# Second MLP's weight pieces loaded from ScalarE's queue, and the decay table loaded between the first q, k and the first k, v

## The chip, the cores and the metric

One core of one Trainium2 chip. The metric is device time in microseconds of one execution, lower is better. The kernel before took 729.98 us, the median of three runs (724.83, 729.98 and 730.90).

## What is computed

Three layers over 2304 tokens of width 512, all in float32 accuracy. The first is retention: attention without a softmax, in which the scores of a head are multiplied by powers of that head's gamma. The second is an MLP (512 to 1024 to 512) with a softmax-like unit and a normalisation in its middle, the third an MLP (512 to 2048 to 512) with a piecewise quadratic unit. Cut to what matters:

```python
scores = scale * q @ k.T                       # 4 batches, 8 heads, 576 tokens, 64 dims
ret = scores * where(i >= j, gamma[h] ** (i - j), 0)
x = heads_joined(ret @ v)                      # 2304 x 512
h = x @ w_in                                   # 512 x 1024
solu = h * softmax(h)
x = ((solu - mean) / sqrt(var + 1e-6) * g_ln) @ w_out
h = x @ moe2_w_in                              # 512 x 2048
g = where(h >= 1, h, where(h <= -1, 0, (h + 1) ** 2 / 4))
out = g @ moe2_w_out                           # 2048 x 512
```

The weights arrive as 64-bit floats, and the kernel turns them into a high and a low 32-bit part itself.

## The kernel before, in words

**Tiles and stages.** The tokens are cut into 18 tiles of 128. Retention runs tile by tile with a running state: `ret_scores` makes the scores (line 115) and multiplies them with the decays inside a tile, `in_sb` (line 124, tile `p`), and scales k by `aft_sb` (line 131); `ret_out` makes the outputs (`po`, lines 143 and 149) and the tile's addition to the state (`pst`, line 170). `mlp1_hidden` multiplies by the first MLP's input weights (`hp`, line 250, twelve matmuls of 512 columns, two halves per token tile; two PSUM buffers), takes a maximum (line 255), and `mlp1_norm` does the softmax and the normalisation: the maxima joined (261), exponentials on ScalarE (265), the product on VectorE (266), which reads `hp` for the last time and so gives its buffer back, and then lines 269 to 283. `mlp1_transpose` (296) and `mlp1_out` (316, 48 matmuls) follow.

**The stretch that the change is about.** A hand-written string, `START`, orders the first steps: L is a load of a tile's q, k (line 104) and k, v (105), C a load of one half of the decays (95), G the other constants, S and O the two retention steps, A and B the first MLP's weights, H and N its hidden and norm. After it a loop runs j from 1 to 8; round j does two token tiles of the first MLP and, in rounds 2 to 5, two tiles of retention. Into the same rounds the second MLP's weights are prepared, in 32 pieces of 512 KB: `prep_load` loads a piece into one of three slots `st` (line 346), and `prep_w2` decodes it: ScalarE copies its two halves (lines 197 and 198), VectorE shifts (199), GpSimd adds (200), VectorE joins (202) and with that the slot is free again; then high and low parts are split off (74 and 75) into a `wi` or `wo` tile, which is stored to DRAM (line 376) for the third layer. `PACE` says how many pieces each of the four places in a round takes. A load of piece k+3 comes right after the decoding of piece k, whose slot it takes.

**What sets the order.** SyncE's instructions stand in the order in which the program makes them, from the first to the last; TensorE's do so from the loop on. ScalarE, VectorE and GpSimd are ordered when the program is built, by a planner that runs the program in a simulated time and takes, of what is ready there, what comes first in the program. At run time every engine goes strictly through its own list. All loads and stores are issued by SyncE, so a load of a piece stands in one row with: the stores of the first MLP's outputs (`store_x2`, line 331, which wait for the splits of `px`), the loads of k, v (105, which wait until `pst` of an earlier tile has read its buffer), and the stores of the prepared weights (376).

**After the rounds** only the second MLP runs (lines 414 to 462), bound by TensorE.

Of the kernel before, what the change touches and what calls it, by code (L numbers as in the profile page):

```python
# [20 lines left out]
B, H, S, D = 4, 8, 576, 64  # L21
T = B * S
DM = H * D
F1, F2 = 1024, 2048
P = 128
# [3 lines left out]
C1, C2 = F1 // P, F2 // P  # L29
# [2 lines left out]
PACE = [[], [0, 0, 0, 0], *[[2, 1, 1, 1]] * 4, *[[2, 2, 1, 1]] * 2, [0, 0, 0, 0]]  # L32

START = """
L0 C1 C0 G0 L1 s0 A0 G1 O0 S1 L2 o1 A1 L3 S2 o2 A2 L4 S3 A3 O3 L5 S4 B0 O4 L6 S5 b1 O5 L7 B2 S6 O6 H0 H1 L8 b3 S7 O7 N0 L9 B4 S8 O8 b5 H2 H3 L10 S9 O9 N1 B6 b7 L11
"""


# [16 lines left out]
def net(ctx: ExitStack, tc: tile.TileContext, qk_t, kv, w_in1, w_out1, g_ln, w_in2, w_out2, inside, before, after, across, out):  # L55
    nc = tc.nc
# [16 lines left out]
    def split(hi, lo, src, eng=nc.vector):  # L73
        nc.scalar.activation(hi, src, AF.Copy)  # L74
        eng.tensor_tensor(out=lo, in0=src, in1=hi.bitcast(F32), op=ALU.subtract)  # L75
# [18 lines left out]
    def load_inside(e):  # L94
        nc.sync.dma_start(in_sb[:, e], inside[:, e])
# [5 lines left out]
    def load_qkv(t):  # L101
        x = raw.tile([P, 2, KD, P], F32, tag="qk", name="qk")
        y = raw.tile([P, 2, H, D], F32, tag="kv", name="kv")
        nc.sync.dma_start(x, qk_t[t])
        nc.sync.dma_start(y, kv[t])
        raws[t] = x, y

# [78 lines left out]
    def words(src, n):  # L186

        return src.bitcast(U32).rearrange("p (f t) -> p f t", t=2)

    def decode(st, tag=None, sb=False, dst=None):  # L190

        lo, hi = st[:, :, 0], st[:, :, 1]
        y = stage.tile([P, 512], U32, tag="y", name="y", bufs=3)
        w = ps.tile([P, 512], U32, tag=tag, name="w") if tag else y
        nc.scalar.activation(w.bitcast(F32), hi.bitcast(F32), AF.Copy, scale=2.0**-112)
        nc.scalar.activation(lo.bitcast(I32), lo, AF.Copy, scale=2.0**-29)  # L198
        nc.vector.tensor_scalar(y, w, 3, None, op0=ALU.logical_shift_left)  # L199
        nc.gpsimd.tensor_tensor(out=y.bitcast(I32), in0=y.bitcast(I32), in1=lo.bitcast(I32), op=ALU.add)  # L200
        r = dst.bitcast(U32) if dst is not None else y if sb else w
        nc.vector.scalar_tensor_tensor(
            out=r, in0=w if tag else hi, scalar=0x80000000, in1=y, op0=ALU.bitwise_and, op1=ALU.bitwise_or
        )
        return r.bitcast(F32)
# [36 lines left out]
    def mlp1_hidden(t, f):  # L242
        xh, xl = x1[t]
        hp = ps.tile([P, 512], F32, tag="o" if t % 2 and (t == 3 or t >= 13) else "h", name="hp")
        fs = slice(f * 512, (f + 1) * 512)
        n = 0
        for kk in range(KD):
            wh, wl = w_in1_sb[kk]
            for a, w in ((xh, wl), (xl, wh), (xh, wh)):
                nc.tensor.matmul(hp, a[:, kk, :], w[:, fs], start=(n == 0), stop=(n == 3 * KD - 1))  # L250
                n += 1
        hps[t, f] = hp
        if f == 0:
            es[t] = (small.tile([P, 12], F32, tag="sm", name="sm"), act1.tile([P, F1], F32, tag=f"e{t % 2}", name="e"))
        nc.vector.tensor_reduce(out=es[t][0][:, f : f + 1], in_=hp, op=ALU.max, axis=AX.X, negate=True)
# [29 lines left out]
    def mlp1_transpose(t):  # L285
        e = es.pop(t)[1]
        if t % 2 == 0:
            ln = act1.tile([P, 2, C1, 2 * P], F32R, tag="ln", name="ln")
            lnT[t // 2] = ln[:, 0], ln[:, 1]
        lh, ll = lnT[t // 2]  # L290
        cols = slice((t % 2) * P, (t % 2 + 1) * P)
        for f4 in range(2):
            tp = ps.tile([P, 4, P], F32, tag="tr", name="tp")
            for j in range(4):
                f = 4 * f4 + j
                nc.tensor.transpose(tp[:, j, :], e[:, f * P : (f + 1) * P], ident)  # L296
            split(lh[:, 4 * f4 : 4 * f4 + 4, cols], ll[:, 4 * f4 : 4 * f4 + 4, cols], tp)
# [31 lines left out]
    def store_x2():  # L329
        for dst, x in xstores:  # L330
            nc.sync.dma_start(dst, x)
        xstores.clear()
# [9 lines left out]
    def prep_load(n):  # L342
        for _ in range(min(n, len(todo))):
            w, i = todo.pop(0)
            st = stage.tile([P, DM, 2], U32, tag="st", name="st")
            nc.sync.dma_start(st, words(w_out2[i * P : (i + 1) * P, :] if w else w_in2[i], DM))
            staged.append((w, i, st))

    def prep_w2(n):

        for _ in range(n):
            w, i, st = staged.pop(0)
            later = [x for x in stores if len(staged) + len(todo) <= x[2] - 2]
            stores[:] = [x for x in stores if x not in later]
            if w == 0:
                x = prep.tile([P, 2, DM], F32R, tag="wi", name="wi", bufs=2)
                split(x[:, 0], x[:, 1], decode(st))
                stores.append((wid[i], x.rearrange("p w (c f) -> p w c f", c=KD), len(staged) + len(todo)))
            elif i % 2 == 0:
                ws[i // 2] = prep.tile([P, 7, 2 * P], F32, tag="ws", name="ws")  # L360
                decode(st, dst=ws[i // 2][:, 0:2].rearrange("p i f -> p (i f)"))
            else:
                y = ws.pop(i // 2)
                decode(st, dst=y[:, 2:4].rearrange("p i f -> p (i f)"))
                for o, a, b in ((4, 1, 0), (1, 3, 1), (5, 3, 4), (6, 2, 5)):
                    nc.gpsimd.tensor_tensor(out=y[:, o], in0=y[:, a], in1=y[:, b], op=ALU.subtract)
                x = prep.tile([P, 2, 7, 2 * P], F32R, tag="wo", name="wo")
                for part in (slice(0, 4), slice(4, 7)):
                    split(x[:, 0, part], x[:, 1, part], y[:, part])
                stores.append((wod[i // 2], x, len(staged) + len(todo)))  # L370
            if len(staged) == 0:
                later += stores
                stores.clear()
            prep_load(1)
            for dst, x, _ in later:
                nc.sync.dma_start(dst, x.bitcast(F32))

# [8 lines left out]
    def load_xs(b, pool):  # L386
        n = blocks[b][1]
        xs[b] = pool.tile([P, 2, KD, n], F32R, tag="ln", name="xs")
        nc.sync.dma_start(xs[b].bitcast(F32), xsd[b])
# [85 lines left out]
    def project_end(b, t):  # L475
# [20 lines left out]

    gs = {}
    start = {
        "L": load_qkv, "C": load_inside, "G": load_consts, "S": ret_scores, "O": ret_out, "A": prep_w_in1, "B": prep_w_out1,
        "H": lambda i: mlp1_hidden(i // 2, i % 2), "N": mlp1_norm, "Y": mlp1_transpose,  # L500
    }
    order = ExitStack()
# [4 lines left out]
    for j in range(1, NT // 2):  # L507
        a = 2 * j
        ra, rb = a + LEAD, a + LEAD + 1
        more = 10 <= ra < NT  # L510
        n = PACE[j]
        mlp1_transpose(a - 2)
        if more:
            ret_scores(ra)
        mlp1_hidden(a, 0)
        mlp1_hidden(a, 1)
        mlp1_norm(a)
        prep_w2(n[0])
        mlp1_transpose(a - 1)
        if more:  # L520
            ret_out(ra)
        prep_w2(n[1])
        store_x2()
        if more:
            ret_scores(rb)
        mlp1_hidden(a + 1, 0)
        mlp1_hidden(a + 1, 1)
        mlp1_norm(a + 1)
        if j == 1:
            pre.close()  # L530
            prep = pre.enter_context(tc.tile_pool(name="prep", bufs=1, side="right", reuse_waits="tile"))
        if more:
            ret_out(rb)
        prep_w2(n[2])
        if more and ra + 2 < NT:
            load_qkv(ra + 2)
        mlp1_out(j - 1, 0)
        if j == 1:
            prep_load(3)
        prep_w2(n[3])  # L540
        if more and rb + 2 < NT:
            load_qkv(rb + 2)
        mlp1_out(j - 1, 1)
        if rb == NT - 1:
            attn.close()
            xsa = ctx.enter_context(tc.tile_pool(name="xsa", bufs=1, side="left", reuse_waits="tile"))
            gsp = ctx.enter_context(tc.tile_pool(name="gsp", bufs=1, side="left", reuse_waits="tile"))
            load_xs(0, xsa)
        if j == 6:
            for c in range(2):  # L550
                load_wi(c, w2a, f"w{c}")
        if j == 7:
            pre.close()
            wos = ctx.enter_context(tc.tile_pool(name="wos", bufs=1, side="right", reuse_waits="tile"))
            for c in range(2, 4):
                load_wi(c, w2a, f"w{c}")
            for s in range(3):
                load_wo(s)
# [78 lines left out]
```

## Time and profile before

| what | value |
|---|---|
| median of three runs | 729.98 us |
| the profiled execution, its own time | 727.76 us |
| its span in the profile | 726.0 us |
| mean granted TensorE clock | 0.979 of full |
| TensorE matmul busy | 688.2 us, 95% |
| VectorE busy | 497.1 us, 68% |
| ScalarE busy | 359.8 us, 50% |
| GpSimd busy | 169.7 us, 23%, all before 330 us |

The profile shows one execution. "Busy" counts computing instructions; issuing a DMA is not counted. An idle stretch is put down to the semaphore that ended it. In a timeline, the bracket at a line's end gives the idle time before the instruction and who ended it. `SPq` and `ACTq` are DMA issues of SyncE and ScalarE; such a line shows the issue, not the transfer. The chain is the work that ended last, followed back from the end.

### The profile page before, as it was taken

The page shows a single profiled execution, that of the slowest core. Times are in us where ns is not written, and L with a number is a line of the kernel's source. Part 1 is how long each engine was busy: PE and PEld are TensorE (multiplying, and loading weights), DVE is VectorE, ACT ScalarE, POOL GpSimd, SP SyncE. Part 2 cuts the span into 40 slices and gives each one's busy share as a digit, 9 for nine tenths or more (in the row PEclk, how much of TensorE's full clock was granted, in tenths as well). Part 3 has the DMA queues.
Part 4 walks back from the last instruction along what each step waited for, and adds up shares of the span by engine and source line. Part 5 has one row for each costly group of instructions (what it writes and reads, how often), then busy time and mean ns, then how long its engine had stood idle before and what let it go on. Part 6 is the DMA issues. An engine that isn't in the chain of part 4 may idle for free.

```text
span 726.0 us, 12169 instructions
## 1 busy us (share of the span) xinstructions
PE 688.2 (95%) x4744; PEld 618.5 (85%) x4744; DVE 497.1 (68%) x961; ACT 359.8 (50%) x658; POOL 169.7 (23%) x186
## 2 busy tenths in 40 slices
PE   5888789998989999999999999999999999999997
PEld 4677578887878889999888989898988899899996
DVE  2977777677588678754566578556865668575875
ACT  2746775575667569763434344333433343343342
POOL 2896645636555235400000000000000000000000
PEclk9989899999999999999999999999999999999999
DMA  8956534487869399699564523346135511555282
GB/s 299 373 185 250 186 116 157 152 324 245 299 224 340 128 356 394 242 391 402 178 242 143 190 89 144 137 184 218 47 125 192 203 59 59 203 193 196 77 320 116
DMA packets 34825, 152.05 MB, mean 209 GB/s; under 512 B 3792, under 2 KB 11984, under 8 KB 29008
## 3 DMA queue, kind: packets, MB, share of 16 engines
q1 hardware_dynamic: 34624, 151.02, 56.8%
q8 instruction: 37, 0.61, 0.3%
q10 hardware_dynamic: 144, 0.26, 0.1%
q14 instruction: 20, 0.16, 0.1%
HBM read 114.04 MB, written 37.22 MB: 208 GB/s over the span
## 4 chain that ended last, share of the span: by engine, by line
PE 72%; DVE 11%; DMA 6%; ACT 4%; POOL 3%; issue 3%; SPq 0%; DVEq 0%; POOLq 0%; ACTq 0%
PE h L414 27%; PE hp L250 9%; PE px L316 7%; PE pa L462 7%; PE pb L462 7%; PE pc L462 7%; PE pd L462 3%; DMA st<-in_w_out 2%; POOL y L200 2%; PE po L149 1%; DMA wod<-wo 1%; PE tp L296 1%; DVE y L199 1%; DVE wo L75 1%; DVE p L124 1%
## 5 line engine op out<-in xcount | busy, mean ns | idle before, releaser
L414 PE MATMUL h<-xs,wi 128*128 128x512 f32 (+1 forms) x960 | 214.2, 372 | 0.0
L414 PEld LDWEIGHTS h<-xs,wi 128*128 128x128 f32 x960 | 163.8, 188 | 28.5
L424 DVE SCALAR_TENSOR_TENSOR r<-r 128x512 f32<-128x512 f32 (+1 forms) x80 | 50.8, 635 | 104.0 <-ACT r L422 103.9
L422 ACT ACTIVATE r<-h 128x512 f32<-128x512 f32 (+1 forms) x80 | 44.4, 555 | 154.7 <-PE h L414 154.6
L74 ACT ACTIVATE gh<-gs 128x1024 fp32r<-128x1024 f32 (+1 forms) x80 | 66.9, 874 | 77.1 <-DVE gs L437 72.9
L316 PE MATMUL px<-ln,wo 128*128 128x256 f32 x864 | 101.4, 278 | 0.0
L316 PEld LDWEIGHTS px<-ln,wo 128*128 128x128 f32 x864 | 100.5, 188 | 0.8 <-ACT e L265 0.2
L250 PE MATMUL hp<-wi1h,x 128*128 128x512 f32 x288 | 96.3, 417 | 0.0
L75 DVE TENSOR_TENSOR gl<-gs,gh 128x1024 fp32r<-128x1024 f32 (+1 forms) x80 | 77.1, 995 | 13.3 <-ACT gh L74 13.2
L200 POOL TENSOR_TENSOR y<-y,st 128x512 int32<-128x512 int32 x48 | 64.2, 1340 | 70.6 <-ACT st L198 22.9
L250 PE MATMUL hp<-wi1l,x 128*128 128x512 f32 x144 | 62.7, 435 | 14.6 <-DVE e L266 12.6
L462 PE MATMUL pb<-wo,gh 128*128 128x256 f32 x288 | 73.9, 280 | 0.4 <-DVE x L75 0.4
L250 PEld LDWEIGHTS hp<-wi1h,x 128*128 128x128 f32 x288 | 58.6, 203 | 13.4
L437 DVE TENSOR_TENSOR gs<-gs 128x256 f32<-128x256 f32 (+1 forms) x160 | 60.0, 396 | 3.6
L462 PE MATMUL pa<-wo,gh 128*128 128x256 f32 x288 | 62.5, 280 | 0.0
L462 PE MATMUL pc<-wo,gh 128*128 128x256 f32 x288 | 62.0, 280 | 0.0
L429 DVE TENSOR_TENSOR gs<-h,r 128x512 f32<-128x512 f32 (+1 forms) x80 | 51.1, 638 | 7.3 <-DVE r L424 0.5
L462 PEld LDWEIGHTS pb<-wo,gh 128*128 128x128 f32 x288 | 54.3, 188 | 0.6 <-issue 0.6
L462 PEld LDWEIGHTS pa<-wo,gh 128*128 128x128 f32 x288 | 49.2, 189 | 2.7
L462 PEld LDWEIGHTS pc<-wo,gh 128*128 128x128 f32 x288 | 49.1, 188 | 0.0
L250 PEld LDWEIGHTS hp<-wi1l,x 128*128 128x128 f32 x144 | 29.4, 204 | 22.6 <-DVE e L266 13.6
L423 ACT COPY h<-h 128x512 f32<-128x512 f32 (+1 forms) x80 | 43.1, 539 | 0.0
(88 smaller groups left out, 1139.0 us busy)
## 6 DMA issues: line engine op xcount, KB each, us to landing
wo<-wod SPq DMA_DIRECT2D x28, 1792.0 KB, 7.4
wod<-wo SPq DMA_DIRECT2D x8, 1792.0 KB, 9.4
st<-in_w_out SPq DMA_DIRECT2D x24, 512.0 KB, 6.1
qk<-in_qk_t SPq DMA_DIRECT2D x18, 512.0 KB, 6.5
kv<-in_kv SPq DMA_DIRECT2D x18, 512.0 KB, 4.5
xsd<-x SPq DMA_DIRECT2D x36, 256.0 KB, 6.4
st<-in_w_in SPq DMA_DIRECT2D x16, 512.0 KB, 6.2
wid<-wi SPq DMA_DIRECT2D x16, 512.0 KB, 7.2
```

Of the source, the lines that this page charges most:

```text
L74: nc.scalar.activation(hi, src, AF.Copy)
L75: eng.tensor_tensor(out=lo, in0=src, in1=hi.bitcast(F32), op=ALU.subtract)
L200: nc.gpsimd.tensor_tensor(out=y.bitcast(I32), in0=y.bitcast(I32), in1=lo.bitcast(I32), op=ALU.add)
L250: nc.tensor.matmul(hp, a[:, kk, :], w[:, fs], start=(n == 0), stop=(n == 3 * KD - 1))
L316: nc.tensor.matmul(px[:, mm, :], w[:, ms], a[:, f, :], start=(n == 0), stop=(n == 3 * C1 - 1))
L414: nc.tensor.matmul(hp[:, :n], wi[c][:, w, kk], xs[b][:, a, kk], start=(k == 0), stop=(k == 3 * KD - 1))
L422: nc.scalar.activation(r[:, :n], hp[:, :n], AF.Relu, bias=0.5, scale=0.5)
L423: nc.scalar.copy(h[:, :n], hp[:, :n])
L424: nc.vector.scalar_tensor_tensor(out=r[:, :n], in0=r[:, :n], scalar=1.0, in1=r[:, :n], op0=ALU.min, op1=ALU.mult)
L429: nc.vector.tensor_tensor(out=g, in0=h_, in1=r_, op=ALU.max)
L437: nc.vector.tensor_tensor(out=g[:, o], in0=g[:, x], in1=g[:, y], op=op)
L462: nc.tensor.matmul(po[key][:, half], a[:, x, t], wo[p][0][:, w, y], start=(begin and j == 0), stop=(last and j == 2), skip_group_check=True,)
```

## The change

Two things. The two halves of the decay table, until now loaded after the first tile's q, k and k, v in the order half 1, half 0, are loaded inside the first tile's load, half 0 then half 1, between q, k and k, v. And the loads of the 32 weight pieces are issued by ScalarE instead of SyncE; two instead of three are issued ahead, and the next one is issued at the beginning of a piece's step instead of after its decoding.

```diff
 START = """
-L0 C1 C0 G0 L1 s0 A0 G1 O0 S1 ...
+L0 G0 L1 s0 A0 G1 O0 S1 ...
 """
@@ load_qkv
         nc.sync.dma_start(x, qk_t[t])
+        for e in range(2 if t == 0 else 0):
+            load_inside(e)
         nc.sync.dma_start(y, kv[t])
@@ prep_load
             st = stage.tile([P, DM, 2], U32, tag="st", name="st")
-            nc.sync.dma_start(st, words(w_out2[i * P : (i + 1) * P, :] if w else w_in2[i], DM))
+            nc.scalar.dma_start(st, words(w_out2[i * P : (i + 1) * P, :] if w else w_in2[i], DM))
             staged.append((w, i, st))
@@ prep_w2
         for _ in range(n):
+            prep_load(1)
             w, i, st = staged.pop(0)
...
             if len(staged) == 0:
                 later += stores
                 stores.clear()
-            prep_load(1)
             for dst, x, _ in later:
                 nc.sync.dma_start(dst, x.bitcast(F32))
@@ start
-        "L": load_qkv, "C": load_inside, "G": load_consts, ...
+        "L": load_qkv, "G": load_consts, ...
@@ the loop over j
         if j == 1:
-            prep_load(3)
+            prep_load(2)
         prep_w2(n[3])
```

## Rows read from the trace of the kernel before

**Rows 1.** The page, fourth part: the chain that ended last, share of the span by engine.
```profile
PE 72%; DVE 11%; DMA 6%; ACT 4%; POOL 3%; issue 3%; SPq 0%; DVEq 0%; POOLq 0%; ACTq 0%
```
**Rows 2.** Busy time by stretch, line 250 alone; after the matmuls: clock, DMA share, GB/s.
```profile
75.00:250.00 175.00, 70.34 (x252) 53.16 (x252) 0.94 0.61 211
250.00:330.00 80.00, 34.89 (x144) 26.60 (x144) 1.00 0.91 350
```
**Rows 3.** Waits of TensorE, whole span: us in total, times, longest.
```profile
PE hp L250 <- DVE e L266: 12.6, 5, 2.8
```
**Rows 4.** The chain that ended last, pieces of 100 to 245 us: start, us, what.
```profile
117.87 5.34 DMA wid<-wi
...
128.56 4.61 PE hp L250 x12
...
139.78 1.18 SPq L346
141.01 9.24 DMA wod<-wo
...
165.21 7.41 PE hp L250 x24
...
237.49 7.41 PE hp L250 x24
```
**Rows 5.** Timeline: SyncE's issues and the VectorE work that frees their slots.
```profile
107.39 1.75 DVE L202 SCALAR_TENSOR_TENSOR ws<-st,y 128x512 uint32<-128x512 uint32 x1
...
109.45 7.86 SPq L331 DMA_DIRECT2D xsd<-x  x4
117.41 0.41 SPq L346 DMA_DIRECT2D st<-in_w_out  x1
...
184.62 7.02 SPq L331 DMA_DIRECT2D xsd<-x  x4
185.24 0.68 DVE L202 SCALAR_TENSOR_TENSOR y<-st,y 128x512 uint32<-128x512 uint32 x1
...
191.73 0.42 SPq L346 DMA_DIRECT2D st<-in_w_in  x1
```
**Rows 6.** Timeline, 196 to 232 us: what follows a late load on three engines.
```profile
196.26 0.68 ACT L197 ACTIVATE y<-st 128x512 f32<-128x512 f32 x1 [5.12 <-DMA st<-in_w_in]
...
197.32 0.68 DVE L255 TENSOR_REDUCE sm<-hp 128x1 f32<-128x512 f32 x1
...
202.36 0.50 PE L250 MATMUL hp<-wi1l,x 128*128 128x512 f32 x1 [2.54 <-DVE e L266]
...
231.44 0.68 ACT L197 ACTIVATE y<-st 128x512 f32<-128x512 f32 x1 [1.24 <-DMA st<-in_w_in]
```
**Rows 7.** The beginning: median landing of DMAs issued before 3 us; chain; timeline.
```profile
kv<-in_kv SPq DMA_DIRECT2D x1, 512.0 KB, 4.5
in_sb<-in_inside SPq DMA_DIRECT2D x2, 256.0 KB, 6.0
...
2.58 5.88 DMA aft_sb<-in_after
...
1.64 0.90 SPq L95 DMA_DIRECT2D in_sb<-in_inside  x2
8.55 0.69 DVE L131 TENSOR_TENSOR kv<-kv,aft_sb 128x512 f32<-128x512 f32 x1 [7.70 <-DMA aft_sb<-in_after]
9.90 0.69 PE L149 MATMUL po<-p,kv 128*64 128x128 f32 x2 [3.28 <-DVE p L124]
14.53 0.33 SPq L105 DMA_DIRECT2D kv<-in_kv  x1
```
**Rows 8.** Waits of ScalarE (78 to 250 us) and of GpSimd (whole span).
```profile
ACT y L197 <- DMA st<-in_w_in: 16.5, 6, 5.1
...
POOL ws L366 <- DVE ws L202: 16.2, 11, 2.5
```
**Rows 9.** Timeline: the only DMA that ScalarE issues before the change.
```profile
722.53 0.38 ACTq L494 DMA_DIRECT2D out<-osb  x1
```

More of the change, by code (lines that the diff above doesn't have):

```diff
@@ L34 @@
 START = """
-L0 C1 C0 G0 L1 s0 A0 G1 O0 S1 L2 o1 A1 L3 S2 o2 A2 L4 S3 A3 O3 L5 S4 B0 O4 L6 S5 b1 O5 L7 B2 S6 O6 H0 H1 L8 b3 S7 O7 N0 L9 B4 S8 O8 b5 H2 H3 L10 S9 O9 N1 B6 b7 L11
+L0 G0 L1 s0 A0 G1 O0 S1 L2 o1 A1 L3 S2 o2 A2 L4 S3 A3 O3 L5 S4 B0 O4 L6 S5 b1 O5 L7 B2 S6 O6 H0 H1 L8 b3 S7 O7 N0 L9 B4 S8 O8 b5 H2 H3 L10 S9 O9 N1 B6 b7 L11
 """
@@ L498, in net @@
     start = {
-        "L": load_qkv, "C": load_inside, "G": load_consts, "S": ret_scores, "O": ret_out, "A": prep_w_in1, "B": prep_w_out1,
+        "L": load_qkv, "G": load_consts, "S": ret_scores, "O": ret_out, "A": prep_w_in1, "B": prep_w_out1,
         "H": lambda i: mlp1_hidden(i // 2, i % 2), "N": mlp1_norm, "Y": mlp1_transpose,
```

## The prediction

> **What bounds the kernel now.** I read the page first. The chain that ended last is TensorE for 72% of the span, VectorE for 11%, transfers for 6%, ScalarE for 4% [rows 1]: the kernel can gain in the 28% where something else holds TensorE up, and where TensorE is slow. The busy time by stretch shows where that is. From 250 us to the end of the first MLP its matmuls follow one another at full clock, 34.89 us for 144, or 0.242 us each; from 75 to 250 us the same 252 matmuls take 70.34 us, 0.279 each, at a granted clock of 0.94 [rows 2]. At the later price they would have taken 61.1, so 9.3 us of that stretch are lost to the lower of the two clock levels. The list of TensorE's waits gives the idle part: five waits, 12.6 us in all and 2.8 at the longest, for VectorE's line 266, which frees the PSUM buffer of `hp` [rows 3]. The chain, read in order of time, shows four of them inside the rounds: TensorE starts again at 128.56, 165.21 and 237.49, each time slowly (4.61 us for 12, 7.41 for 24, where 12 and 24 at the later price take 2.9 and 5.8) [rows 4], and at 202.36 after 2.54 us of idling [rows 6]. The fifth lies ahead of these. Before each gap the chain runs over VectorE, ScalarE, stores and loads of weight pieces, so the preparation of the second MLP's weights is what TensorE ends up waiting for.
>
> Next, the timeline of SyncE's queue. A load needs a free slot, and it needs its turn. The slot of the load issued at 117.41 was freed by the join that began at 107.39 and took 1.75, so at 109.1; the load stood 8.3 us behind four stores of `px` outputs. That of 191.73 had its slot from 185.24 + 0.68 = 185.9 on, and stood 5.8 us behind the next such four [rows 5]. ScalarE then waits for the landing with everything behind it: six waits, 16.5 us [rows 8].
>
> **Start.** The same bytes change places. Now k, v land 4.5 us after an issue just ahead of the decays' 1.64, so near 5.7, and the second half of the decays near 2.1 + 6.0 = 8.1; `aft_sb` lands at 2.58 + 5.88 = 8.46, and VectorE, which has the scaling of k first in its list, begins at 8.55, does the decays behind it and lets `po` begin at 9.90 [rows 7]. With the places changed I expect decays near 6 and k, v near 8.1; VectorE can then multiply the decays in while it waits, and `po` begins when v is there, near 8.3. That is 1.6 us; I take **-1.5**. It is passed on, because the third tile's k, v load stands at 14.53 until `po` has read its buffer [rows 7], and the first weights are issued behind it. Bounds: nothing, if the planner leaves the scaling of k first; +0.9, the issue time of the two halves, if k, v and not `aft_sb` then end that wait.
>
> **Loads off SyncE's queue.** The distance does not change: piece k+2 issued before the decoding of k, and k+3 issued after it, both take the slot that was freed last. What goes is the time behind other transfers. By gaps:
> - 202.36: late load, ScalarE's copy at 196.26 after a wait of 5.12 us, VectorE's shift behind it, and so the second maximum only at 197.32; then exponentials, product, TensorE [rows 6]. With the load issued some 5 us earlier the copy doesn't wait and the gap closes: **-2.5**. Next comes TensorE's own work.
> - 237.49: the copy at 231.44 waited 1.24 us for a load of the same kind [rows 6]; the rest is VectorE's own queue. **-1.2**.
> - 165.21: the chain comes here from a store of prepared weights at 141.01, 9.24 us long, which was issued behind a load that held SyncE for 1.18 [rows 4]. The store stays on SyncE but has no load ahead of it: **-1.2**.
> - 128.56: the chain comes from a store issued at 117.87, behind the load of 117.41 [rows 4, 5]. The four stores before both stay: **-0.5**.
> - Clock: three of these gaps are followed by some 1.7 us of slowness (4.61 against 2.9, 7.41 against 5.8) [rows 2, 4]. I count one of the three as saved, **-1.7**; bounds 0 and -5.0.
>
> Together -7.1. The bounds: 0, if all these gaps have VectorE's queue as their true cause, and all four gaps whole. These are 2.54 where the wait stands [rows 6], for the other three at most 2.8 each [rows 3], and the clock's 5.0: -16.
>
> **What ScalarE pays.** It issues 32 DMAs more. Its only one now takes 0.38 us [rows 9], so 12 us. In the rounds it has idle time of its own to hide them, of which the 16.5 us of waiting for landings alone [rows 8] is more. Behind a load stand the exponentials and splits of its list. ScalarE holds 4% of the chain, 29 us [rows 1], and the rounds and the start, where most of this must lie, last some 330 us: a tenth. A tenth of the 12 us is 1.2; I take **+1.0**, between 0 and 12. The wait for the slot moves to ScalarE as well: for a piece with a following split ScalarE waits for the same join anyway, so it costs little; for the others see the third rival.
>
> After 330 us nothing of the change runs. Behind 250 us TensorE is dense [rows 2], so an earlier start there is kept.
>
> The issuing rule of the Trainium skill speaks against this change: its page "DMA: Bandwidth & Descriptors", section "Issuing engines are not separate DMA queues", says that DMAs started by several engines share the same 16 DMA engines, and that a second issuer saves only the issuing time. By that rule alone the sum would be the second rival's time. No row of this case shows how two issuers share the engines; but the 8.3 and 5.8 us lie before the issue [rows 5], which the rule doesn't count.
>
> **Sum.** -1.5 - 7.1 + 1.0 = -7.6. The profiled execution took 727.76 us itself (726.0 of span and 1.8 around it), which makes 720.2. The runs' median of 729.98 lies 0.3% higher, so 722.4 in its measure; I give **722**. A measurement of this kernel can tell about 1% from no change, 7.3 us, so this stands just at that edge.
>
> **Rivals.**
> 1. *All gaps close.* Once loads come on time, decoding is over before the maxima, and all four gaps go with their clock: 727.76 - 1.5 - 16 = 710.3, in the median's measure 712. For it: every gap is preceded by preparation work. Against: the stores at 117.87 and 141.01, which the chain goes through, stay in SyncE's order. Chance 0.13.
> 2. *The load was hidden anyway.* VectorE's queue and the stores set the gaps, and only the start's 1.5 us stay, less ScalarE's 1.0: 727.3, or 729.5. For it: two of the four gaps come over stores. Against: the straight line from late load to gap at 202.36. That the change doesn't do what it says belongs here: the planner may place the load on ScalarE's list no earlier than SyncE had it. Chance 0.27.
> 3. *ScalarE stands in front of the exponentials.* A load in its list waits until VectorE's join frees the slot, and line 265 waits behind it, which frees `hp`. GpSimd, which waits for that join today, did so 11 times, 16.2 us, 1.5 each [rows 8]. With the issue that is 1.9 us a stand. If two stands per round meet the exponentials in rounds 2 to 5, that is 15.2 and the clock's 5.0 on top, without gain from the loads: 727.76 - 1.5 + 20.2 = 746.5, or 749 in the median's measure; with half of it 739. It decides when ScalarE's waits at its loads exceed the 16.5 us that it now waits for landings. Against: the planner puts the load where the slot is free by its own reckoning. Chance 0.12.
>
> **How the numbers follow.** Forecast 0.48, rivals 0.13, 0.27, 0.12. The range 711 to 739 reaches from the first rival to half of the third; the forecast's own is 716 to 727. Faster by over 1%, that is below 722.7: half of the forecast's cases and the first rival, with some beyond, 0.42. Slower by over 1%: the third rival, 0.12. Within 1%: 0.46.
>
> **What would show it.** Right: ScalarE's waits for `st` landings before 250 us fall from 16.5 us to below 6; loads are issued within 2 us of their slot's join; the gap near 202 is gone, and TensorE's waits for line 266 sum to 6 to 9 us; `po` begins near 8.3 us. Wrong: loads still late, which is the second rival; waits of ScalarE at the new load line of 10 us or more with longer gaps at `hp`, the third; or the gaps as before though the loads come early, which would say that VectorE's queue was the cause.

## The result, and the profile after

The kernel after takes **736.87 us** (median of ten runs, 732.71 to 740.72); the kernel before, in ten runs beside it, 726.7 us. The ratio is 1.0136, with a 95% interval of 1.0106 to 1.0167. The forecast was 722, and faster. The number lies in the range of 711 to 739, but on the wrong side of no change.

The profiled execution of after has a span of 735.0 us, 9.0 more than before. Its page, the engines' busy time, then the landings of the pieces' loads (the last number is the median from issue to landing, in us):

```profile
PE 685.0 (93%) x4744; PEld 615.3 (84%) x4744; DVE 502.7 (68%) x961; ACT 360.4 (49%) x658; POOL 170.2 (23%) x186
...
st<-in_w_in ACTq DMA_DIRECT2D x16, 512.0 KB, 4.5
st<-in_w_out ACTq DMA_DIRECT2D x16, 512.0 KB, 3.9
```

TensorE, ScalarE and GpSimd are busy within 3.2 us of before and VectorE for 5.6 us more; the mean granted clock is 0.985 against 0.979. So TensorE is not slower, it idles more. Before, the loads of these pieces landed 6.2 and 6.5 us after their issue; now 4.5 and 3.9:

```profile
st<-in_w_in SPq DMA_DIRECT2D x16, 512.0 KB, 6.2
st<-in_w_out SPq DMA_DIRECT2D x16, 512.0 KB, 6.5
```

So the edit did what it says, and the loads are quicker. They also leave on time: 27 of the 29 that need a freed slot are issued within 2 us of the join that frees it, where before it was 10.

The loss is made in the rounds: the last `px` matmul starts at 361.7 us, against 352.7 before, which is the whole 9.0; behind it the two kernels run alike. Taken at the first matmul of a tile's `hp`, the changed kernel is still level at 164.8 us (165.2 before), 4.7 us behind at 193.7, 7.2 at 231.6 and 9.4 at 246.9.

TensorE's waits of after from 75 to 330 us (us in total, times, longest):

```profile
PE hp L252 <- DVE e L268: 9.0, 4, 3.2
PE px L318 <- DVE state L179: 5.0, 1, 5.0
PE tp L298 <- ACT e L285: 3.3, 1, 3.3
PE hp L252 <- DVE y L204: 3.2, 2, 2.5
PE tp L298 <- DVE ln L75: 2.7, 3, 1.6
PE tp L298 <- DVE x L75: 2.1, 1, 2.1
PE px L318 <- DVE state L185: 1.2, 1, 1.2
```

Line 268 is line 266 of before; all lines from 105 on are two higher. The sum is 26.5 us, 27.5 with `po`'s, against 16.6 before, where beside the 12.6 of [rows 3] there were only these two:

```profile
PE hp L250 <- DVE y L202: 2.1, 1, 2.1
PE tp L296 <- ACT e L283: 1.9, 1, 1.9
```

The wait for line 266 (now 268) has fallen from 12.6 to 9.0. What has grown are the waits of `px` and `tp`, for the state, for the normalised tile and for splits: 14.3 us together, 1.9 before. And ScalarE, from 75 to 330 us:

```profile
ACT st L200 <- DMA st<-in_w_out: 14.8, 5, 5.4
...
ACT st L200 <- DMA st<-in_w_in: 7.8, 4, 4.2
...
ACT y L199 <- DMA st<-in_w_in: 4.8, 2, 3.7
```

The waits for landings have not fallen. They have moved from a piece's first copy (line 199, 197 before: 21.8 us in this stretch then, most of it in [rows 8]) to its second (line 200, 198 before: 2.0 us then). The second copy works in place on the low words, so it needs no `y` buffer, and nothing can use it until the first copy has run too. In the list of ScalarE's instructions as built, 21 of the second MLP's 32 second copies stand ahead of their own first copy; before it was 5. The planner has laid ScalarE's row anew.

The largest new wait, in the timeline from 161 to 185 us. Each line is start, duration, engine and line; the bracket is the idle time before it and what ended it:

```profile
161.79 0.35 ACTq L348 DMA_DIRECT2D st<-in_w_out  x1
162.25 0.42 SPq L378 DMA_DIRECT2D wod<-wo  x1
162.98 0.33 SPq L104 DMA_DIRECT2D qk<-in_qk_t  x1
164.14 0.33 ACTq L348 DMA_DIRECT2D st<-in_w_in  x1
...
170.85 0.67 ACT L200 ACTIVATE st<-st 128x512 int32<-128x512 uint32 x1 [5.39 <-DMA st<-in_w_out]
171.42 0.71 ACT L275 ACTIVATE junk<-e,sm 128x512 bf16<-128x512 f32 x1
...
176.46 0.67 ACT L200 ACTIVATE st<-st 128x512 int32<-128x512 uint32 x1 [4.23 <-DMA st<-in_w_in]
177.02 0.71 ACT L275 ACTIVATE junk<-e,sm 128x512 bf16<-128x512 f32 x1
177.85 0.21 DVE L279 TENSOR_SCALAR sm<-sm 128x1 f32<-128x1 f32 x1 [7.40 <-ACT junk L275]
...
182.06 0.69 DVE L268 SCALAR_TENSOR_TENSOR e<-hp,e 128x512 f32<-128x512 f32 x1 [2.36 <-ACT e L267]
...
183.47 0.85 DVE L179 COPY state<-pst 64x256 f32<-64x256 f32 x2
...
184.47 7.29 PE L318 MATMUL px<-ln,wo 128*128 128x256 f32 x48 [5.04 <-DVE state L179]
```

Read it upwards. TensorE waits 5.04 us for VectorE to empty `pst`. VectorE stands in its own row 7.40 us at line 279, a step of 0.21 us that adds up the two squares of a normalisation. The squares (line 275) are ScalarE's: the first at 171.42, the second at 177.02, and between them a second copy that waits 4.23 us for a piece. VectorE stands another 2.36 us at line 268 for exponentials that come behind all this in ScalarE's row. Before, nothing stood between that pair of squares:

```profile
169.48 0.72 ACT L273 ACTIVATE junk<-e,sm 128x512 bf16<-128x512 f32 x1
170.33 0.72 ACT L273 ACTIVATE junk<-e,sm 128x512 bf16<-128x512 f32 x1
```

The same happens at 223 us, where two squares are 4.4 us apart with a landing waited for in between. The kernel before has one such pair, at 179 us, 4.35 us apart.

Why the pieces land late just there is in the DMA list, issues from 160 to 166 us:

```profile
wod<-wo SPq DMA_DIRECT2D x1, 1792.0 KB, 14.0
st<-in_w_out ACTq DMA_DIRECT2D x2, 512.0 KB, 6.3
kv<-in_kv SPq DMA_DIRECT2D x1, 512.0 KB, 9.1
qk<-in_qk_t SPq DMA_DIRECT2D x1, 512.0 KB, 14.6
st<-in_w_in ACTq DMA_DIRECT2D x1, 512.0 KB, 12.3
```

The load of 164.14 is issued right after the join that frees its slot (163.43 + 0.68), and lands 12.3 us later, beside a store of 1792 KB and two more pieces. In these 6 us the kernel before issued the same store, q, k and k, v, but one piece where there are now three: 3328 KB against 4352. At the 306 GB/s of the next line 4352 KB take 14.6 us, which is an estimate. DMA share and rate of 162 to 176 us:

```profile
162.00:176.00 14.00, 12.11 (x93) 10.47 (x92) 8.31 (x19) 4.48 (x10) 7.48 (x10) 1.00 0.91 306
```

Before, the same 14 us had a DMA share of 0.69 and 245 GB/s.

### The profile page after: what moved, and what is told of

It is laid out like the page before. It is cut to its first block, busy times and chain, and to the rows that moved or that the text cites. A ratio compares the mean times of both kernels' runs of the same rounds, so it can differ in the third digit from the quotient of the medians.

```text
span 735.0 us, 12160 instructions
## 1 busy us (share of the span) xinstructions
PE 685.0 (93%) x4744; PEld 615.3 (84%) x4744; DVE 502.7 (68%) x961; ACT 360.4 (49%) x658; POOL 170.2 (23%) x186
## 4 chain that ended last, share of the span: by engine, by line
PE 58%; DVE 5%; DMA 2%; ACT 1%; issue 1%; DVEq 0%; SPq 0%; ACTq 0%
PE h L416 27%; PE pa L464 7%; PE pb L464 7%; PE pc L464 7%; PE px L318 4%; PE pd L464 3%; PE hp L252 3%; DMA wod<-wo 2%; PE tp L298 1%; DVE ln L75 1%; DVE gl L75 1%; DVE wo L75 1%; DVE sm L257 1%; DVE ws L204 0%; DVE e L268 0%
## 5 line engine op out<-in xcount | busy, mean ns | idle before, releaser
L318 PE MATMUL px<-ln,wo 128*128 128x256 f32 x864 | 102.9, 280 | 6.2 <-DVE state L179 5.0
L252 PE MATMUL hp<-wi1h,x 128*128 128x512 f32 x288 | 92.3, 402 | 0.0
L75 DVE TENSOR_TENSOR gl<-gs,gh 128x1024 fp32r<-128x1024 f32 (+1 forms) x80 | 77.0, 995 | 13.6 <-ACT gh L74 13.5
L252 PE MATMUL hp<-wi1l,x 128*128 128x512 f32 x144 | 60.1, 418 | 12.4 <-DVE e L268 9.0
L252 PEld LDWEIGHTS hp<-wi1h,x 128*128 128x128 f32 x288 | 55.7, 193 | 12.3
L200 ACT ACTIVATE st<-st 128x512 int32<-128x512 uint32 x48 | 32.1, 671 | 25.1 <-DMA st<-in_w_out 16.0
```

What stands on the lines that cost most here:

```text
L318: nc.tensor.matmul(px[:, mm, :], w[:, ms], a[:, f, :], start=(n == 0), stop=(n == 3 * C1 - 1))
```

## The experiments

Each ratio is to the kernel before, run beside it on the same chip, with its 95% interval. Each version was run ten times, but the loads alone, the loads on GpSimd, the same hold with SyncE, the fourth slot and the held loads four times. "After with" means the changed kernel with one more edit.

### Which part of the change it is

**The start alone.** The decays' order as changed; the pieces' loads stay on SyncE, three ahead.

```diff
-L0 C1 C0 G0 L1 s0 A0 G1 O0 S1 ...
+L0 G0 L1 s0 A0 G1 O0 S1 ...
+        for e in range(2 if t == 0 else 0):
+            load_inside(e)
```

> Only the start's order is changed; the weight pieces are loaded by SyncE as before. Theory A (ScalarE stands at landings that come late, because the planner puts a piece's copies right behind a load that now shares the DMA engines with a store of prepared weights): within 2 us of before, ratio 0.997 to 1.003, waits of ScalarE for st landings between 110 and 250 us near before's 18 us. Theory C (the changed start makes the planner lay out the rounds anew, and that is the loss): +7 to +11 us, ratio 1.010 to 1.015.

Measured: 1.0008 (0.9977 to 1.0039). The start is worth nothing.

**The loads alone.** From ScalarE, two ahead; the start as before.

```diff
-            nc.sync.dma_start(st, ...)
+            nc.scalar.dma_start(st, ...)
+            prep_load(1)
...
-            prep_load(1)
...
-            prep_load(3)
+            prep_load(2)
```

> Only the loads are moved to ScalarE, two ahead; the start is as before. Theory A: +7 to +11 us, ratio 1.010 to 1.015, with single waits of ScalarE for st landings of 4 us or more in the rounds and TensorE waits at px or tp that before has not. Theory C: within 2 us of before.

Measured: 1.0148 (1.0112 to 1.0185), which is the whole loss. ScalarE waits at the second copies again (10.9 + 9.1 us).

**After with the loads on SyncE.** The new place in the step, two ahead, the old queue.

```diff
-            nc.scalar.dma_start(st, ...)
+            nc.sync.dma_start(st, ...)
```

> As the changed kernel, but the loads are issued by SyncE, at the new place (two ahead, before the decoding). Theory A: about before's time, ratio 0.995 to 1.004, since the loads stay in SyncE's row and finish in the order of their issue. Theory D (the new place in the step, not the queue, is the loss): ratio 1.010 or more. If ScalarE's issuing is the loss (theory B), about before's time as well.

Measured: 0.9956 (0.9934 to 0.9978): faster than the kernel before. Only 6 second copies stand ahead of their first, and the waits for landings sit at the first copies (11.5 + 6.0 us). The new place in the step is a gain (from 1.0008 with the start alone), and the queue is the loss. In SyncE's row the new place is a later one: the load that takes the same slot now stands behind the stores of the step before it, where it stood ahead of them. That this is what gains is argued from the program; no run holds the two apart.

**After with the loads on GpSimd.**

```diff
-            nc.scalar.dma_start(st, ...)
+            nc.gpsimd.dma_start(st, ...)
```

> As the changed kernel, but the loads are issued by GpSimd. SyncE's row is as free as with ScalarE, and ScalarE issues nothing. Theory A: the landings are as late and the copies on ScalarE stand as before, so still slower than before, ratio 1.005 to 1.02. Theory B (the 32 issues on ScalarE and its waits for slots are the loss): ratio 1.000 or lower.

Measured: 1.0187 (1.0140 to 1.0235). ScalarE issues nothing here, so its issuing isn't needed for a loss of this size. But the run is no clean mirror. 18 second copies stand early again, and GpSimd itself now stands 34.5 us at the loads, for their slots:

```profile
POOL st L348 <- DVE ws L204: 34.5, 6, 15.0
```

### Where ScalarE stands for a landing

**After with both copies held.** Each of a piece's two copies must stand behind ScalarE's instruction that is traced ahead of it. For the first copy that is the load of the piece two on, for the second it is the first copy.

```diff
-        nc.scalar.activation(w.bitcast(F32), hi.bitcast(F32), ...)
-        nc.scalar.activation(lo.bitcast(I32), lo, ...)
+        first = nc.scalar.activation(w.bitcast(F32), hi.bitcast(F32), ...)
+        if pin: tc.keep_in_program_order(first)
+        second = nc.scalar.activation(lo.bitcast(I32), lo, ...)
+        if pin: tc.keep_in_program_order(second)
```

> As the changed kernel, but in the preparation of the second MLP's weights the two copies of a piece are kept in ScalarE's list behind what the program makes ahead of them, so the planner can't put them in front of a normalisation. Theory L (the list: with loads off SyncE's row the planner takes the pieces as landed early and puts their copies in front of ScalarE's work for the norm, where they stand until the landing): the loss goes, ratio 0.990 to 1.004, and TensorE's waits at px and tp go. Theory S (sharing: loads off SyncE's row land late and make q, k, k, v and stores land late, wherever the copies stand): still 1.008 or more.

Measured: 0.9956 (0.9935 to 0.9977). The loss is gone, with the loads still on ScalarE's queue. ScalarE's waits from 75 to 330 us: the two new ones, which are for a slot (the load ahead of the copy waits for the join that frees it), and the only one left for a landing, which is a copy of the first MLP's weights:

```profile
ACT y L199 <- DVE ws L208: 11.4, 4, 4.2
ACT y L199 <- DVE y L208: 4.5, 2, 3.3
...
ACT w L199 <- DMA st<-in_w_out: 2.2, 1, 2.2
```

TensorE's waits in the same stretch fall to 14.9 us, and none is for the state or a split:

```profile
PE hp L256 <- DVE e L272: 10.6, 5, 3.2
PE hp L256 <- DVE y L208: 3.3, 1, 3.3
PE tp L302 <- ACT e L289: 1.0, 2, 0.6
```

**The same hold, with the loads on SyncE.** Both edits above together.

> The loads issued by SyncE two ahead, with the start of the changed kernel, and the same two copies kept in program order. Theory L: SyncE's row already keeps the pieces near their place, so little changes against the same kernel without it: 0.990 to 1.000 of before. If keeping the order is costly by itself: above 1.004.

Measured: 1.0632 (1.0588 to 1.0676); a clear miss. With no load on ScalarE's list, the first copy is held behind ScalarE's compute of the same step, which comes late. Slots come free late, and SyncE's row stands at the loads, 184.6 us in all from 75 to 330 us (before: 58.0), 45 of them at 85 us, with q, k and k, v behind them; TensorE then waits 11.1 us for q, k. SyncE's three largest waits there (us in total, times, longest), then the longest of its issues:

```profile
SPq L352 <- DVE y L208: 83.9, 7, 44.3
SPq L352 <- DVE ws L208: 54.2, 6, 21.4
SPq L352 <- DVE sm L283: 27.4, 3, 11.8
```
```profile
84.98 45.01 SPq L352 DMA_DIRECT2D st<-in_w_out  x2
```

**After with a fourth slot**, three ahead (another pool gives up a buffer for it).

```diff
-    stage = ...tile_pool(name="stage", bufs=3, ...)
+    stage = ...tile_pool(name="stage", bufs=4, ...)
-    small = ...tile_pool(name="small", bufs=4, ...)
+    small = ...tile_pool(name="small", bufs=3, ...)
-            prep_load(2)
+            prep_load(3)
```

> As the changed kernel with four slots for pieces instead of three, three loads ahead (and three instead of four small tiles of the norm, for room). Theory S, and any theory in which the lead is too short: the pieces are there when the copies come, the loss goes, ratio 0.990 to 1.004. Theory L: the planner uses the lead to put the copies still earlier, and ScalarE stands as long: ratio 1.008 to 1.02.

Measured: 1.0247 (1.0191 to 1.0302). More lead makes it worse: 30 of 32 second copies now stand early. If late loads were the trouble, a slot more should have helped. The small tile that the norm lost could cost as well, and no run took it away alone; but line 257, which takes such a tile, waits only for its matmuls here, 6.7 us against 6.4 in after.

**After with the loads held** behind what is traced ahead of them on ScalarE.

```diff
-            nc.scalar.dma_start(st, ...)
+            tc.keep_in_program_order(nc.scalar.dma_start(st, ...))
```

> As the changed kernel, but the loads, not the copies, are kept in program order in ScalarE's list, so they are issued later. Theory L: the planner counts the pieces as landed later and the copies fall behind the norm's work; ratio 0.995 to 1.006. Theory S: the loads land later still and ScalarE stands longer; ratio 1.012 or more.

Measured: 1.0395 (1.0343 to 1.0447); a miss. The first load comes at 105.2 us instead of 76.4, everything of the preparation comes late, and SyncE stands at the stores of prepared weights, 168.6 us for three releasers, of which two are the splits of line 75 (78.8 and 69.3).

So this run says nothing on copies that stand early; it shows what a late load costs.

### Is it the early second copy as such

**After with only the second copy held**, behind its own first. No second copy of the second MLP then stands early.

```diff
+        if pin: tc.keep_in_program_order(second)
```

> The changed kernel, with only the second of a piece's two copies on ScalarE held behind its own first copy (the first copy is as free as in the changed kernel). In ScalarE's row of the changed kernel 21 of the second MLP's 32 second copies stand ahead of their own first copy (5 in the kernel before, 6 with the same loads issued by SyncE, 18 by GpSimd, 30 with a fourth slot), and nothing waits for such a copy until the first has run too. Theory F (the early second copies are the loss): ScalarE's waits for landings at the second copy, 22.6 us from 75 to 330 us, fall under 5 us, the wait of px for the state goes, and the time is 0.990 to 1.003 of the kernel before. Theory G (any copy that stands early costs as much; the first copies now take the waits over): the first copies wait 20 us or more and the time stays at 1.008 or above.

Measured: 1.0036 (1.0006 to 1.0066). Three quarters of the loss go. The waits are now 13.3 us, all at first copies; the longest, 5.8 us, stands ahead of a norm's pair of squares, and none inside one. The time lies just above theory F's 1.003; its other two signs are there, no wait for a landing at the second copies and none of `px` for the state.

**After with only the first copy held**, the second free.

```diff
+        if pin: tc.keep_in_program_order(first)
```

> The changed kernel, with only the first of the two copies held behind ScalarE's instruction traced ahead of it (the load of the piece two on), and the second free. In ScalarE's row 31 of 32 second copies then stand ahead of their first. Theory F (the early second copies are the loss): the second copies wait 20 us or more for landings from 75 to 330 us and the time is 1.010 to 1.030. Theory G (the place of the first copy decides, and holding it is what mended the run with both held): the time is at most 1.002.

Measured: 1.0016 (0.9992 to 1.0040), where the early second copies as such should have cost 1.0% or more. 31 of 32 stand early, and ScalarE waits for them as long as in after:

```profile
ACT st L202 <- DMA st<-in_w_in: 15.8, 6, 4.5
...
ACT st L202 <- DMA st<-in_w_out: 6.8, 7, 2.0
```

So neither the count nor the sum of the waits makes the loss. The time is the one that theory G gave, at most 1.002: the place of the first copy bears on the loss too. It does not decide alone, since holding only the second gave back three quarters. In the timeline the two longest of these waits stand ahead of a pair of squares: at 175 and 213 us, where they last 4.4 and 4.5 us, both squares follow 0.85 us apart. One pair is parted, 4.43 us at 197, but VectorE has other work ahead of the step that needs it and stands there for little:

```profile
202.53 0.21 DVE L281 TENSOR_SCALAR sm<-sm 128x1 f32<-128x1 f32 x1 [1.47 <-ACT junk L277]
```

In the changed kernel that step (line 279 there) stood 7.40 us.

**Loads on SyncE, only the second copy held.**

> Loads two ahead from SyncE's queue, and only the second copy held behind its first. Both held took 1.063: SyncE stood 176 us at the loads for their slot from 75 to 330 us. Theory H (there the first copy was held behind the norm's work of the same step, which comes late, and the slots with it): with the first copy free SyncE stands under 30 us at the loads and the time is 0.988 to 1.000, as with nothing held (0.996). Rival (any held copy keeps the slots): SyncE stands over 100 us and the time is 1.03 or more.

Measured: 0.9975 (0.9942 to 1.0008). SyncE stands 50.0 us at the loads (184.6 with both held, 58.0 before), 14.6 + 8.8 of them for the joins, so the bound of 30 holds for the joins only; the 6% of the run with both held are gone. It was the held first copy that stopped the slots.

**The kernel before, second copy held.**

> The kernel before, with the second copy held behind its first. Only 5 of 32 stood ahead of it and they wait 2.0 us from 75 to 330 us, where the first copies wait 21.8 us. Theory F: 0.996 to 1.004, the copies' waits as before. Rival (holding the copies is a gain of its own, which is all that made the changed kernel with both held faster than before): 0.994 or less.

Measured: 1.0028 (1.0003 to 1.0053). Holding the copies is no gain of its own.

### One square for both halves

A norm's two squares of 512 columns become one of 1024, so that nothing can stand between them, in the changed kernel and in the kernel before:

```diff
-        for f in range(2):
-            junk = act1.tile([P, 512], BF16, ...)
-            nc.scalar.activation(junk, ef, AF.Square, ..., accum_out=sm[:, 8 + f : 9 + f])
+        junk = act1.tile([P, F1], BF16, ...)
+        nc.scalar.activation(junk, e, AF.Square, ..., accum_out=sq)
...
-        nc.vector.tensor_scalar(sq, sq, sm[:, 9:10], 1.0 / F1, op0=ALU.add, op1=ALU.mult)
-        nc.vector.tensor_scalar(sq, sq, esum, None, op0=ALU.add)
+        nc.vector.tensor_scalar(sq, sq, 1.0 / F1, esum, op0=ALU.mult, op1=ALU.add)
```

> The changed kernel, with the norm's two squares of 512 columns made one of 1024 (its sum goes to one column, and VectorE's two small steps behind it become one), so that no copy can stand between the two halves. Theory P (what costs is a copy of a piece, and its wait for a landing, between the two squares of one norm: 5.6 us from one square to the next at 171 and 4.4 at 223 in the changed kernel, 0.85 where nothing stands between): against the kernel before with the same edit the time is within 0.5%, and px doesn't wait for the state. Theory Q (a wait ahead of the pair costs as much as one inside it): the changed kernel stays 1.0% or more above the kernel before with the same edit. The edit itself saves some 0.3 us on ScalarE and one small step on VectorE per norm, for both kernels alike.

> The kernel before, with the norm's two squares of 512 columns made one of 1024. It is the reference of the run of the changed kernel with the same edit. Both theories: 0.990 to 1.002 of the kernel before (16 norms, each at most 0.5 us shorter on ScalarE and VectorE, most of it beside TensorE's work; the one pair parted by 4.4 us at 179 closes under theory P, which gives up to 0.4%).

Measured: 1.0046 (1.0023 to 1.0068) and 0.9975 (0.9953 to 0.9996). Between the two that is 0.71% (1.0046 / 0.9975), where the kernels as they are differ by 1.36%. Taken straight from the ten runs of each, which ran on one chip, it is 0.87% (medians 730.86 and 724.57). So between a third and a half of the loss goes, between the two expectations, and with intervals of 0.2% to 0.3% on each ratio the share is rough. `px` waits 0.7 us for the state, where it was 6.2. The edit also changes what the planner lays out, so it need not act on the squares alone; 23 second copies still stand early. The longest wait for a landing now stands ahead of a norm. In the changed kernel with one square:

```profile
168.74 0.67 ACT L200 ACTIVATE st<-st 128x512 int32<-128x512 uint32 x1 [6.74 <-DMA st<-in_w_out]
169.31 1.14 ACT L273 ACTIVATE junk<-e,sm 128x1024 bf16<-128x1024 f32 x1
```

### What the runs say together

Sums of waits from 75 to 330 us, each from one profile; ScalarE's are those for landings of weights (up to 2.5 us of each are the first MLP's). The profiled execution can lie off the median: that of the fourth slot took 740.54 us with a median of 745.43, that with the loads on SyncE 720.83 with 723.87.

| kernel | ratio | ScalarE, us | TensorE, us |
|---|---|---|---|
| before | 1 | 25.0 | 16.6 |
| after | 1.0136 | 29.6 | 27.5 |
| loads alone | 1.0148 | 28.9 | 24.2 |
| fourth slot | 1.0247 | 25.7 | 27.0 |
| one square, after | 1.0046 | 26.4 | 22.5 |
| second copy held | 1.0036 | 15.7 | 21.9 |
| first copy held | 1.0016 | 24.1 | 17.1 |
| one square, before | 0.9975 | 29.2 | 16.8 |
| loads on SyncE | 0.9956 | 22.5 | 12.8 |
| both copies held | 0.9956 | 2.2 | 14.9 |

ScalarE's column doesn't follow the time; TensorE's does, roughly. A wait of ScalarE costs what stands behind it in the row and is needed by an engine that TensorE waits for.

One number of the traces does set the versions apart: the time from the later of a piece's two copies to its join, as the mean of the 32 pieces. It is 3.7 to 4.4 us in the eight versions from 0.9956 to 1.0028, and 6.5 to 8.3 in the six from 1.0036 to 1.0247 (after: 7.3, before: 4.1); the two runs in which everything comes late, 1.0395 and 1.0632, have 4.3 and 3.6. With the first copy held it is 4.4, with one square 6.9. Whether this makes the loss or only goes with it, no run shows.

**Shown:** the loss comes with the queue of the loads, not with the start and not with the new place in the step; the loads on ScalarE's queue cost nothing when the copies are held, and holding either copy takes most of the loss away; making a norm's two squares one takes away between a third and a half. **Argued:** that the planner moves the copies forward because in its simulated time a load that waits behind nothing lands early. It fits the counts of early second copies (6 with SyncE, 21 with ScalarE, 18 with GpSimd, 30 with one slot more), but the simulated times were not read. **Open:** what the rest is made of (waits ahead of the norms, or pieces that stay longer in their slots), and how much of the 12.3 us landing is due to the store and how much to the two pieces beside it; no run took either away.

Two versions beat both kernels by the same amount: the changed kernel with the loads on SyncE, and the changed kernel with both copies held, 0.9956 each. The kernel before with one square, 0.9975, also lies below before, by little.

## Why the prediction was wrong

**The step that failed** is the one that makes up the gaps' share of the forecast, "Together -7.1", and its first term above all: "With the load issued some 5 us earlier the copy doesn't wait and the gap closes: **-2.5**". It takes the place of the copies in ScalarE's row as given, and counts what a new row would cost at nothing. That row is laid by the planner when the program is built, and it came out anew. The loads do come on time, and this gap does close: the same matmul, 2.54 us late at 202.36 before [rows 6], follows without a wait.

```profile
204.64 0.50 PE L252 MATMUL hp<-wi1l,x 128*128 128x512 f32 x1
```

Whether the earlier load closed it, or the 4.7 us that TensorE is late by then, these rows do not tell. And the copies wait as long as ever, at worse places: their waits for `st` landings, 78 to 250 us, are 27.1 us (13.7 + 7.8 + 4.8 + 0.8) where I wrote below 6 for right. The 16.5 of the prediction was one line of the list; all four lines were 21.2 before (16.5 + 2.7 + 1.2 + 0.8). TensorE gains 3.6 us at line 268, within the 6 to 9 us that I wrote for right, and loses 12.4 at `px` and `tp`, which the sum did not have.

The gap at 202 was also no measure of the load's worth. The chain of before does not pass through it: from 176 us on it runs over loads, ScalarE, VectorE and GpSimd, the load of 191.73 among them, and meets TensorE again only at 237.49.

**Bounds of the trace:** right. The rounds decide, and after 330 us nothing of the change runs: the 9.0 us stand already at the last `px`.

**Start, -1.5:** nothing (1.0008). It came out at the bound named for it: the planner left the scaling of k first, and it now waits 8.18 us, where it was 7.70, for `aft_sb`, which is issued at 2.58 us as before. `po` begins at 10.39 where it was 9.90 [rows 7], not at 8.3, and the third tile's k, v load stands at 14.55 where it was 14.53:

```profile
9.04 0.69 DVE L133 TENSOR_TENSOR kv<-kv,aft_sb 128x512 f32<-128x512 f32 x1 [8.18 <-DMA aft_sb<-in_after]
...
10.39 0.69 PE L151 MATMUL po<-p,kv 128*64 128x128 f32 x2 [3.83 <-DVE p L126]
```

**Loads off SyncE's queue, -7.1:** the sum was mis-sized too. The two fastest versions give 0.44%, 3.2 us of 726.7, and one of them leaves the loads on SyncE. So what can be had came from the new place in the step, and leaving SyncE's queue added nothing that these runs can tell. The sentence "The distance does not change" had dismissed just that place. With both copies held no piece's copy waits for a landing and all 29 loads that need a freed slot are issued within 0.8 us of its join, and TensorE still waits 10.6 us for the line that was 266, 12.6 before; the gap at 202 is there again, 3.16 us long. ScalarE had stood for the slot ahead of it instead:

```profile
187.28 0.69 ACT L199 ACTIVATE y<-st 128x512 f32<-128x512 f32 x1 [3.35 <-DVE y L208]
...
193.37 0.79 PE L256 MATMUL hp<-wi1l,x 128*128 128x512 f32 x1 [3.16 <-DVE e L272]
```

So this is the case that the prediction named last, the gaps nearly as before though the loads come early. Its reading of that case, VectorE's queue as the cause, fits in so far as the slot is freed by VectorE's join; no run tests it by itself.

**Clock, -1.7:** it is no part of the loss. From 75 to 250 us the granted clock is 0.96 where it was 0.94, and line 252's matmuls take 62.14 us for 241, 0.258 each, against 0.279 [rows 2]. For 252 of them that is 5.3 us, an estimate from the two rows and more than the term; it was lost again elsewhere:

```profile
75.00:250.00 175.00, 62.14 (x241) 47.03 (x242) 0.96 0.63 221
```

**ScalarE pays, +1.0:** an issue takes 0.34 us, near the 0.38 of [rows 9]. That 32 of them cost next to nothing is borne out by the version with both copies held, which issues them all and is as fast as the one with the loads on SyncE.

**The rivals.** The first is 25 us off: three of its four gaps are still there, 1.95, 1.89 and 2.00 us long. The third had the right sign and engine, and with 739 for its half a time 2 us off, which is luck. Its mechanism is not what happened. ScalarE's idle time straight ahead of its loads, from the records of the issues, is 13.5 us in after, under the 16.5 from which it was to decide, and TensorE's waits for `hp` have not grown; the version with both copies held has 25.7 us of it and is faster than before, the one with the first copy held has 11.0. GpSimd, as the issuer, did stand so, 34.5 us. The second rival's reason was met only in the start.

By the rule that the prediction cites from the Trainium skill ("DMA: Bandwidth & Descriptors", section "Issuing engines are not separate DMA queues") the time would have been the second rival's; the measurement is slower than that. What it says of sharing agrees with the 12.3 us that a load of ScalarE's took beside SyncE's store.

## What to carry to other kernels

Where a planner lays an engine's row, moving a DMA to another queue is also an edit of that row: compare the rows as built before forecasting, and look for instructions that nobody needs yet and that now stand, waiting for a landing, ahead of some that are needed. Don't sum an engine's waits; ask of each what stands behind it in the row and who needs that. Holding such instructions in the program's order can mend it, but what they are held behind decides whether that gains 0.4% or costs 6%.

## What the hardware showed that I had not expected

In one stretch the transfers that two engines issued within 2 us of each other landed nearly together: the store of 1792 KB at 162.25 took 14.0 us, q, k of 512 KB at 162.98 took 14.6, the piece of 512 KB at 164.14 took 12.3, where such a piece takes 4.5 or 3.9 as the median. So they landed within 1.3 us, and the load, with a queue of its own, no sooner than the store that was issued 1.9 us ahead of it. Among the transfers of one engine the order of issue held: from 60 to 340 us none of SyncE's 92 or ScalarE's 32 in after, and none of SyncE's 128 in before, landed ahead of the one issued before it.
